# Delta-rule recurrence and expert layer on one core: eight units per substitution, a second transposition of K, and unread transposes on TensorE

## The chip, the cores and the metric

The kernel runs on one core of one Trainium2 chip. The metric is device time in microseconds, median over runs. Engines are named as in the profile: PE (TensorE matmuls), PEld (TensorE weight loads), DVE (VectorE), ACT (ScalarE), POOL (GpSimd), SP (SyncE, which here only issues DMAs). Everything is float32.

## The reference

Two blocks follow each other. The first is a delta-rule recurrence over 768 tokens for 4 batches of 8 heads of width 48. Keys are normalised, and a 48x48 state per head is updated token by token:

```
k_n = k / (norm(k) + 1e-6)
for t in range(768):
    y[t]  = q[t] @ state
    v_old = k_n[t] @ state
    state = state + beta[t] * outer(k_n[t], v[t] - v_old)
```

The second is a mixture of experts over the 3072 resulting rows of width 384. A cosine router picks one of eight experts for each row (argmax of normalised row times normalised expert embedding, over tau, with the softmax probability of the winner as gate), and the row becomes `gate * (relu(x @ w1[e]) @ w2[e])` with a hidden width of 1024.

## The kernel before

**Tiling of the recurrence.** The sequence is cut into 12 chunks of 64 tokens (C = 64, chunk m). A unit n = 2m + i is one chunk for two of the four batches and all their heads, so there are 24 units and two chains, i = 0 and 1, each with its own state S. Four units (two chunks, m = 2g and 2g + 1) are a group g; there are six. Inside a chunk the token-by-token update is a triangular system of size 64. It is split into halves of 32 (HC). The inverses of the 32x32 diagonal blocks are found by substitution on DVE: all blocks of a group lie one to a partition, and 30 steps of two instructions each (a product into tmp, a subtraction from X) work through them.

**Preparation of a group** (function `prepare`): K is loaded (`planned_k`, eight DMAs for a chunk), squared on ACT, summed on DVE, its root taken (ACT for groups 0 and 1, a POOL power later), scaled (`keys`, on POOL but for chunk 1), transposed on PE in eight 128x128 transposes (`transposes`, helper `turned`, L309), and copied out of PSUM by ACT into the K half of the buffer KQ. `gram_diag` forms the diagonal Gram blocks of a chunk from KQ in 64 small products of 48x32; `to_lanes` (L546) transposes them on DVE so that each block gets a partition; `lower` masks them on POOL; `product` (L561) and `subtract` (L565) are the substitution; `from_lanes` (L573) transposes back, and two ACT copies (`spread`) write W, which the group's units need for their solves.

**A unit** (function `unit`): a Gram of K against K and Q (PE), masked into Sx (ACT) and M (DVE, L652); then the chain: `old` (PE), R = V - old (DVE, L670), `solve` (PE), Y (ACT), `fix` (PE), U (ACT), `solve_again` (PE), Z (ACT), `update` (PE), state (DVE, L719). Beside it run `from_state` and `inside` (PE), which give the unit's output XC, its transposition, and the router's logits. After every fourth unit (twice at the end) `routing` chooses experts and puts tokens on lists in DRAM through POOL. `queries` loads and transposes q of a chunk into the Q half of KQ; `values` loads v and scales it on POOL into V (L615).

**Early tiles.** When the 16th unit is done, expert 0 already takes two tiles of 128 of its tokens (`early_tile`); their products are interleaved with the last units.

**What sets the order.** All of the recurrence is written as tasks, `plan.add(engine, busy, more, key, run, reads, writes, take, mode, hold)`: a planned busy time, a latency, a due time (key, in periods of 7.5 from the group's or unit's place), what it reads and writes, and whether it takes one of four PSUM pairs. `Plan.order` runs the tasks through its own list schedule and so fixes each engine's order; `emit` then issues the instructions in that order. Engines work their queues in order, so a waiting instruction holds what stands behind it. `with_warmers` holds a loop that never runs (`while False`), so no unread product is issued.

**The expert stage** starts when the recurrence's buffers are free: up to 31 tiles of 128 tokens, 26 of which run here, each a gather (POOL), a transposition, 24 and 8 products (PE), a ReLU copy (ACT), the gating (DVE) and a scatter (POOL). Weights stream through SP's queue.

Of the kernel before, what the change touches and what calls it, by code (L numbers as in the profile page):

```python
# [11 lines left out]
ALU = mybir.AluOpType  # L12
# [4 lines left out]
C = 64  # L17
HC = 32
T = 128
# [5 lines left out]
WARM = 0.45  # L25
# [3 lines left out]
class Plan:  # L29
# [77 lines left out]
    def with_warmers(self, order):  # L107
        out, last = [], 0.0
        for t, i in order:
            if self.tasks[i][0] == "PE":  # L110
                at = last + 0.15
                while False:
                    out.append((at, -1))
                    at += WARM
                last = self.ends[i]
            out.append((t, i))
        return sorted(out, key=lambda x: x[0])

    def emit(self, warm):
        free, left = list(range(len(self.psum))), dict(self.users)  # L120
        for _, i in self.with_warmers(self.order()):
            if i < 0:
                if free:
                    warm(self.psum[free[0]])
                continue
            _, _, _, _, run, _, take, of, _, _ = self.tasks[i]
            if take:
                self.held[take] = free.pop(0)
            run()
            for a in of:  # L130
                left[a] -= 1
                if not left[a]:
                    free.append(self.held[a])
# [6 lines left out]
def kernel(  # L140
# [80 lines left out]
    buffers("v", 3, [2, H, D])  # L221
    buffers("sq", 1, [2, H, D])
    buffers("K", 6, [2, H, C])
    buffers("KQ", 5, [2, NP, 2, 2 * C])
# [3 lines left out]
    rings["X"], rings["WT"] = carved(2, [HC, HC], w2_flat), carved(3, [HC, HC], w2_flat)[2:]  # L228
    buffers("tmp", 2, [(HC // 2) * (HC // 2)])
    buffers("W", 2, [HC, C])  # L230
# [93 lines left out]
    flat_buffers("V", 3, 4 * NP * D)  # L324
# [75 lines left out]
    def beta_refine(part):  # L400
# [5 lines left out]
             writes=["ident", "half", "iotas"] + [("K", i) for i in range(6)] + [("q", i) for i in range(2)])  # L406
# [14 lines left out]

    def prepare(g):
        ms = (2 * g, 2 * g + 1)
        t0 = group_key(g)
# [59 lines left out]
        for part in (slice(0, 1), slice(1, 2)) if g == 0 else (slice(0, 2),):  # L484
            xs = range(part.start, part.stop)
            those, roots_of = [at("rn", g) + (x,) for x in xs], [at("rt", g) + (x,) for x in xs]
            if g < 2:
                plan.add(*act(16 * len(xs)), t0 - 10 * PERIOD, roots_act(part), reads=those + ["half"], writes=roots_of)
            else:
                plan.add("POOL", 5.5, 0.2, t0 - 10 * PERIOD, roots(part), reads=those + ["half"], writes=roots_of)  # L490
            plan.add("DVE", 1.1 if g < 2 else 0.5, 0.2, t0 - 9.6 * PERIOD - (g == 0) * 30, scales(part), hold=g == 0,
                     reads=those, writes=roots_of + ["quots"])
            plan.add("DVE", 0.12 * len(xs), 0.2, t0 - 9.6 * PERIOD, scaled(part), hold=g == 0,
                     reads=[("sqb", 2 * g + x) for x in xs], writes=roots_of)

# [8 lines left out]
        def transposes(src, m, name):  # L504
            def step():
                turned(pair((name, m)), buf(src, m))
            return step

        def out_of_psum(m, name, cols):
            def step():  # L510
                act_copy(buf("KQ", m).rearrange("d i j y c -> d (i j y) c")[:, :, cols],
                         pair((name, m)).rearrange("d i (x c) -> d (i x) c", c=C))
            return step

        def gram_diag(m):
            def step_():
                p = pair(("diag", g))
                KQ = buf("KQ", m)
                for step in range(2 * NP):
                    for y in range(2):  # L520
                        for hf in range(2):
                            for jj in range(2):
# [6 lines left out]
                                mm(p[r:r + HC, jj, to:to + w], KQ[rows, i, j, y, hf * HC:(hf + 1) * HC], KQ[rows, i, j, y, c:c + w])  # L529
            return step_  # L530
        for m in ms:
            plan.add(*(dve(850) if m == 1 else pool(768)), t0 - 9.2 * PERIOD + (m % 2) * PERIOD, keys(m), hold=g == 0,
                     reads=[("k", m % 4, 0), ("k", m % 4, 1), at("rt", g) + (m % 2,)], writes=[at("K", m)])
            plan.add(*pe(8, 0.11), t0 - 8.6 * PERIOD + (m % 2) * PERIOD, transposes("K", m, "KT"), mode=2,
                     reads=[at("K", m), "ident"], take=("KT", m))
            plan.add(*act(1024), t0 - 8.4 * PERIOD + (m % 2) * PERIOD, out_of_psum(m, "KT", slice(0, C)),
                     reads=[("psum", ("KT", m))], writes=[at("KQ", m) + ("K",)])
        for m in ms:
            first = m % 2 == 0
            plan.add(*pe(64, 0.02), t0 - 7.2 * PERIOD, gram_diag(m), mode=1, reads=[at("KQ", m) + ("K",)],  # L540
                     writes=[("X_next", g % 2)] + ([] if first else [("psum", ("diag", g))]),
                     take=("diag", g) if first else None)
        X = buf("X", g)

        def to_lanes():
            nc.vector.transpose(X, pair(("diag", g)).rearrange("p jj (x c) -> p c jj x", c=HC))  # L546
        plan.add(*dve(1024), t0 - 6.5 * PERIOD, to_lanes, hold=g == 0, reads=[("psum", ("diag", g))],
                 writes=[at("X", g), ("X_next", g % 2)])
# [5 lines left out]
        plan.add("POOL", 1.2, 0.1, t0 - 6.4 * PERIOD, lower, writes=[at("X", g)])  # L554

        for j in range(1, HC - 1):
            rows = HC - 1 - j
            t = buf("tmp", j)[:, 0:rows * j].rearrange("p (a b) -> p a b", b=j)

            def product(j=j, rows=rows, t=t):  # L560
                nc.vector.tensor_tensor(t, X[:, j + 1:, j:j + 1].broadcast_to([128, rows, j]),  # L561
                                        X[:, j:j + 1, 0:j].broadcast_to([128, rows, j]), op=ALU.mult)

            def subtract(j=j, rows=rows, t=t):
                nc.vector.tensor_tensor(X[:, j + 1:, 0:j], X[:, j + 1:, 0:j], t, op=ALU.subtract)  # L565
            key = t0 - (6.0 - j * 4.0 / HC) * PERIOD
            plan.add("DVE", rows * j / 960 + 0.085, 0.13, key, product, reads=[at("X", g)], writes=[at("tmp", j)], hold=g == 0)
# [728 lines left out]
```

## Time and profile before

| | |
|---|---|
| median of 14 runs | 660.07 us (656.65 to 667.39) |
| the profiled execution | 658.53 us, of which the profile's span is 656.8 us |
| PE busy | 555.1 us, 85% of the span, 9995 instructions |
| DVE busy | 266.6 us, 41% |
| ACT busy | 180.3 us, 27% |
| POOL busy | 167.4 us, 25% |
| last product of the early tiles ends | 352.7 us |
| first product of the expert stage | 357.3 us |

Times in the profile count from the start of the span. A group line has the source line, engine, operation and tiles, the shape and number, then the busy time in us and the mean of one in ns, then the engine's idle time just before them and what ended it. PEclk is the share of TensorE's clock that was granted. A float32 product shows as two passes, so 16 products are x32; a transpose is one. Tile names that share storage are shown under one name: w_first stands for X as well as for K's load buffer, since both are carved from the first weights' storage.

### The profile page before, as it was taken

How to read it: one execution, taken by the hardware profiler on the slowest of the kernel's cores; microseconds unless marked ns; L12 is line 12 of the kernel's file. 1: busy time of each engine (PE TensorE's matmuls, PEld its weight loads, DVE VectorE, ACT ScalarE, POOL GpSimd, SP SyncE). 2: the span in 40 equal slices, each digit the busy share in tenths (PEclk: the TensorE clock that was granted, in tenths of full speed). 3: DMA queues.
4: the chain of work that ended last, by engine and by line, in shares of the span. 5: the costliest groups of instructions: out<-in, count | busy, mean ns of one | idle time of the engine just before them, and what ended most of it. 6: DMA issues, size and time to landing. Idle time of an engine off the chain costs nothing. (4 is left out here: it accounts for less than half of the span.)

```text
span 656.8 us, 22729 instructions
## 1 busy us (share of the span) xinstructions
PE 555.1 (85%) x9995; PEld 464.2 (71%) x9995; DVE 266.6 (41%) x749; ACT 180.3 (27%) x327; POOL 167.4 (25%) x217
## 2 busy tenths in 40 slices
PE   3563687777888887777996999999999999999991
PEld 3452676666787877676874878787878787878780
DVE  4798769679769777533214011111111111111100
ACT  2222625537427345263330101110101010101010
POOL 4434334354242121302203212121212121211100
PEclk9985769589869769799798999999999999999996
DMA  4444744534214311222002999999899999999600
GB/s 76 77 80 80 193 76 80 118 71 83 78 29 100 86 49 26 79 78 78 31 2 77 370 390 391 390 341 344 293 343 319 335 312 332 336 322 329 208 24 7
DMA packets 127911, 115.46 MB, mean 176 GB/s; under 512 B 83754, under 2 KB 113873, under 8 KB 127810
## 3 DMA queue, kind: packets, MB, share of 16 engines
q1 hardware_dynamic: 122242, 102.93, 51.0%
q0 software_dynamic: 4480, 10.85, 4.5%
q8 instruction: 80, 1.31, 0.8%
q10 hardware_dynamic: 1088, 0.20, 0.2%
q14 instruction: 21, 0.17, 0.1%
HBM read 102.02 MB, written 12.72 MB: 175 GB/s over the span
## 5 line engine op out<-in xcount | busy, mean ns | idle before, releaser
L1164 ACT ACTIVATE hT<-acc 128x512 f32<-128x512 f32 x52 | 31.1, 597 | 258.7 <-PE acc L1162 251.2
L1162 PEld LDWEIGHTS acc<-xTm,w 128*128 128x128 f32 x816 | 93.8, 192 | 4.5
L1162 PE MATMUL acc<-xTm,w 128*128 128x128 f32 x816 | 93.9, 275 | 0.0
L1169 PE MATMUL acc<-w,hT 128*128 128x384 f32 x272 | 90.5, 486 | 0.0
L1172 POOL DMA_INDIRECT out_dram<-y,ids x26 | 26.3, 1011 | 205.7 <-DVE y L1171 187.3
L1169 PEld LDWEIGHTS acc<-w,hT 128*128 128x128 f32 x272 | 50.4, 190 | 31.5
L273 PE MATMUL psum_pair<-KQ 48*32 48x64 f32 (+2 forms) x2304 | 53.5, 275 | 20.8 <-issue 10.4
L1154 DVE COPY xTm<-acc 128x384 f32<-128x384 f32 x26 | 14.5, 558 | 135.1 <-PE acc L1153 135.1
L565 DVE TENSOR_TENSOR w_first<-w_first,tmp 128x30 f32<-128x30 f32 (+9 forms) x180 | 67.8, 378 | 3.9
L561 DVE TENSOR_TENSOR tmp<-w_first 128x30 f32<-128x30 f32 (+9 forms) x180 | 66.8, 373 | 4.1
L1171 DVE TENSOR_SCALAR y<-acc,xg 128x384 f32<-128x384 f32 x26 | 16.1, 618 | 125.0 <-PE acc L1169 125.0
L273 PEld LDWEIGHTS psum_pair<-KQ 48*32 48x32 f32 (+1 forms) x2304 | 43.6, 139 | 28.7 <-issue 15.5
L1162 PEld LDWEIGHTS acc<-xTm,w_first 128*128 128x128 f32 x432 | 51.6, 198 | 3.3 <-DVE xTm L1154 1.2
L1162 PE MATMUL acc<-xTm,w_first 128*128 128x128 f32 x432 | 51.8, 282 | 0.8 <-DVE xTm L1154 0.8
L1169 PE MATMUL acc<-w_first,hT 128*128 128x384 f32 x144 | 47.9, 486 | 0.0
L273 PE MATMUL psum_pair<-S,KQ 48*64 48x64 f32 x1408 | 37.4, 247 | 10.0 <-issue 4.5
L273 PEld LDWEIGHTS psum_pair<-S,KQ 48*64 48x64 f32 x1408 | 31.7, 157 | 13.6 <-issue 6.8
L1169 PEld LDWEIGHTS acc<-w_first,hT 128*128 128x128 f32 x144 | 26.7, 190 | 16.7
L276 ACT ACTIVATE KQ<-psum_pair 128x1024 f32<-128x1024 f32 x24 | 24.4, 1023 | 47.1 <-PE psum_pair L309 34.3
L1137 POOL DMA_INDIRECT xg<-x_dram,ids x26 | 25.3, 975 | 38.5 <-DMA ids<-idmap 22.4
L960 POOL DMA_INDIRECT idmap<-tokid,slots_i x24 | 24.1, 1005 | 42.9 <-DVE slots_i L936 13.8
L615 POOL TENSOR_TENSOR V<-v,sqb 128x384 f32<-128x384 f32 x24 | 20.6, 863 | 51.1 <-DVE R L670 33.9
(183 smaller groups left out, 744.9 us busy)
## 6 DMA issues: line engine op xcount, KB each, us to landing
w<-in_moe_w_dram SPq DMA_DIRECT2D x34, 1536.0 KB
w_first<-in_moe_w_dram SPq DMA_DIRECT2D x16, 1536.0 KB
q<-in_q_dram SPq DMA_DIRECT2D x96, 48.0 KB
v<-in_v_dram SPq DMA_DIRECT2D x48, 96.0 KB
w_first<-in_k_dram SPq DMA_DIRECT2D x88, 48.0 KB
x_dram<-XC SPq DMA_DIRECT2D x5, 800.0 KB
idmap<-space SPq DMA_DIRECT2D x1, 2048.0 KB
w_first<-in_moe_w_dram SPq DMA_DIRECT2D x6, 256.0 KB
```

The lines of the kernel that those rows point to most:

```text
L273: nc.tensor.matmul(out_, lhsT=lhsT, rhs=rhs, start=start, stop=True, skip_group_check=True)
L276: nc.scalar.activation(out_, in_, ACT.Copy, scale=scale)
L561: nc.vector.tensor_tensor(t, X[:, j + 1:, j:j + 1].broadcast_to([128, rows, j]), X[:, j:j + 1, 0:j].broadcast_to([128, rows, j]), op=ALU.mult)
L565: nc.vector.tensor_tensor(X[:, j + 1:, 0:j], X[:, j + 1:, 0:j], t, op=ALU.subtract)
L615: nc.gpsimd.tensor_tensor(buf("V", m)[:, i * 2 * NP * D:(i + 1) * 2 * NP * D].rearrange("p (jj j d) -> p jj j d", jj=2, d=D), buf("v", m)[ ...
L960: put = nc.gpsimd.indirect_dma_start(out=idmap[:, :], out_offset=bass.IndirectOffsetOnAxis(ap=slot_i[:, i:i + 1], axis=0), in_=K["tokid"][ ...
L1137: t.read = nc.gpsimd.indirect_dma_start(out=t.x, out_offset=None, in_=x_dram[:, :], in_offset=bass.IndirectOffsetOnAxis(ap=t.ids[:, 0:1], ...
L1162: nc.tensor.matmul(psH[:, i, :], lhsT=t.w1[:, j, (f + i) * 128:(f + i + 1) * 128], rhs=t.xT[:, j, :], start=(j == 0), stop=(j == KC - 1))
L1164: nc.scalar.activation(t.hT[:, f:f + 4, :], psH, ACT.Relu)
L1169: nc.tensor.matmul(psO, lhsT=t.hT[:, f, :], rhs=t.w2[:, f, :], start=(f == 0), stop=(f == NF - 1))
L1171: nc.vector.tensor_scalar_mul(y, psO, t.x[:, Dm:Dm + 1])
L1172: nc.gpsimd.indirect_dma_start(out=out[:, :], out_offset=bass.IndirectOffsetOnAxis(ap=t.ids[:, 1:2], axis=0), in_=y, in_offset=None, bound ...
```

## The change

1. **Substitution of eight units at once.** Groups are solved in lanes `[[0], [1], [2, 3], [4, 5]]`. X becomes one tile with two halves, and for a pair each instruction covers both halves, so the 30 steps are issued four times and not six. Groups 2 and 3, and 4 and 5, are prepared together, ahead of the earlier one's first unit.
2. **K transposed separately for the diagonal Gram.** `prepare` transposes K into a buffer KT of its own (two of them, one carved from `space[0]`) for `gram_diag`; `queries` transposes K again, together with q, into KQ shortly before the chunk's units.
3. **Buffers.** v goes from three to two, V from three to two, KQ from five to three, tmp from two to one (twice as long), K from six to eight, W from two to three.
4. **Unread transposes.** `emit` looks at the plan: where PE is planned to wait more than 0.3 us before a task, and that task takes a PSUM pair or one is free, it issues up to six 128x128 transposes of the identity into that pair ahead of the task. Nothing reads them. In the built kernel these are 196 in 43 places.

```
-WARM = 0.45
+MOST = 6
...
-        free, left = list(range(len(self.psum))), dict(self.users)
-        for _, i in self.with_warmers(self.order()):
...
+        free, left, last = list(range(len(self.psum))), dict(self.users), 0.0
+        for t, i in self.order():
+            engine, _, _, _, run, _, take, of, _, _ = self.tasks[i]
             if take:
                 self.held[take] = free.pop(0)
+            if engine == "PE":
+                if t - last > 0.3 and (take or free):
+                    warm(self.psum[self.held[take] if take else free[0]], min(MOST, int((t - last) / 0.12)))
+                last = self.ends[i]
             run()
...
-    buffers("v", 3, [2, H, D])
+    buffers("v", 2, [2, H, D])
-    buffers("K", 6, [2, H, C])
-    buffers("KQ", 5, [2, NP, 2, 2 * C])
+    buffers("K", 8, [2, H, C])
+    buffers("KQ", 3, [2, NP, 2, 2 * C])
+    buffers("KT", 1, [2, NP, 2, C])
+    rings["KT"] += carved(1, [2 * NP, 2 * C], space[0])
-    rings["X"], rings["WT"] = carved(2, [HC, HC], w2_flat), carved(3, [HC, HC], w2_flat)[2:]
-    buffers("tmp", 2, [(HC // 2) * (HC // 2)])
-    buffers("W", 2, [HC, C])
+    X2, rings["WT"] = carved(1, [2, HC, HC], w2_flat)[0], carved(3, [HC, HC], w2_flat)[2:]
+    buffers("tmp", 1, [2 * (HC // 2) * (HC // 2)])
+    buffers("W", 3, [HC, C])
-    flat_buffers("V", 3, 4 * NP * D)
+    flat_buffers("V", 2, 4 * NP * D)
...
+    LANES = [[0], [1], [2, 3], [4, 5]]
+    lanes_of = {g: those for those in LANES for g in those}
...
-        t0 = group_key(g)
+        those = lanes_of[g]
+        t0 = group_key(those[0]) - (3.5 - those.index(g)) * (len(those) > 1) * PERIOD
...
+    def substitute(those):
+        two = len(those)
+        lo = those[0] % 2 if two == 1 else 0
+        X = X2[:, lo:lo + two]
+        names = [("X", lo + x) for x in range(two)]
+        t0, step = group_key(those[0]), (4.0 if two == 1 else 7.0) / HC * PERIOD
         for j in range(1, HC - 1):
             rows = HC - 1 - j
-            t = buf("tmp", j)[:, 0:rows * j].rearrange("p (a b) -> p a b", b=j)
+            n = two * rows * j
+            t = buf("tmp", j)[:, 0:n].rearrange("p (s a b) -> p s a b", s=two, b=j)
...
-                nc.vector.tensor_tensor(X[:, j + 1:, 0:j], X[:, j + 1:, 0:j], t, op=ALU.subtract)
+                nc.vector.tensor_tensor(X[:, :, j + 1:, 0:j], X[:, :, j + 1:, 0:j], t, op=ALU.subtract)
...
+        for src, first, of in (("K", 0, [at("K", m)]), ("q", C, [at("q", m) + (i,) for i in range(2)] + [("q", m % 2)])):
+            def transposes(src=src):
+                turned(pair((src, "T", m)), buf(src, m))
...
+            plan.add(*pe(8, 0.11), t0 - 3.5 * PERIOD + first / C, transposes, mode=2, reads=of + ["ident"], take=(src, "T", m))
...
-    prepare(0)
+    def prepare_lanes(those):
+        for g in those:
+            prepare(g)
+        substitute(those)
+        for g in those:
+            if g != 5:
+                out_of_lanes(g)
+    prepare_lanes([0])
...
-        if g + 1 < NG:
-            prepare(g + 1)
+        if g + 1 < len(LANES):
+            prepare_lanes(LANES[g + 1])
+        if g == 3:
+            out_of_lanes(5)
...
-    def warm(p):
-        for b in range(2):
-            mm(p[HALF[b], b, 0:256], ident[:, HALF[b]], half_wide)
+    def warm(p, n):
+        for _ in range(n):
+            nc.tensor.transpose(p[:, 0, 0:128], ident, ident)
     plan.emit(warm)
```

## The prediction

> **What bounds the kernel now.** I read the slices of the page first, for the stages; then the busy time in stretches, for the engine that is full in each; then the groups, for prices; then the timeline, for steps.
>
> ```profile
> PE   3563687777888887777996999999999999999991
> ...
> DVE  4798769679769777533214011111111111111100
> ...
> PEclk9985769589869769799798999999999999999996
> ```
>
> A slice is 16.4 us. DVE is busy six to nine tenths up to the 16th slice and almost idle from the 18th; PE is nearly full from the 23rd. The granted clock dips in the first half alone. So there are two stages: the recurrence up to 353 us, where the last early product ends, and the experts after it (304 us, PE 20.00 of 20 us in most stretches), which the change doesn't touch. What it is worth is how much earlier the first stage ends.
>
> Stretches (length; busy PE, PEld, DVE, ACT, POOL; then the granted clock):
>
> ```profile
> 90.00:96.00 6.00, 5.12 (x76) 4.67 (x79) 3.73 (x9) 1.09 (x2) 3.58 (x3) 0.50 0.51 90
> 180.00:186.00 6.00, 5.54 (x154) 5.05 (x155) 2.55 (x6) 1.02 (x1) 2.26 (x4) 0.50 0.20 37
> ...
> 198.00:204.00 6.00, 4.69 (x229) 4.25 (x228) 5.75 (x18) 4.68 (x6) 1.62 (x2) 1.00 0.32 56
> 228.00:234.00 6.00, 5.61 (x236) 4.90 (x236) 3.97 (x11) 1.52 (x2) 1.87 (x3) 0.50 0.52 124
> 258.00:264.00 6.00, 4.80 (x183) 4.51 (x177) 5.69 (x20) 3.57 (x8) 1.89 (x2) 1.00 0.01 3
> 288.00:294.00 6.00, 4.33 (x197) 3.89 (x197) 1.16 (x2) 4.25 (x11) 0.00 (x0) 1.00 0.13 37
> ```
>
> The bound changes hands. At 1.00 DVE is full (5.75, 5.69 of 6) and PE is not; at 0.50 PE is full and DVE waits (2.55, 3.97). In stretches of 1 us the clock is 0.50 in nine stretches before 353 us, 109 us in all. After 284 us, where the last substitution ends, neither is full: there the chain of a unit (PE, copy, PE, copy) sets the pace.
>
> Two sums measure this. **DVE:** its queue, priced by the rows' means with 33 ns between instructions, up to the last transposition of groups 0 to 5: 50.6, 92.9, 130.7, 165.9, 200.3, 235.8 us; the trace has them at 63.8, 113.7, 160.0, 201.4, 241.5, 284.2. So DVE waited 13, 21, 29, 36, 41, 48 us by then. **PE:** its queue to 353 us at full clock is 236 us by steps such as these:
>
> ```profile
> 183.03 1.99 PE L273 MATMUL psum_pair<-S,KQ 48*64 48x64 f32 x64
> 184.91 1.13 PE L273 MATMUL psum_pair<-R,W 64*64 64x64 f32 x32
> ...
> 329.76 0.69 PE L273 MATMUL psum_pair<-R,W 64*64 64x64 f32 x32
> 330.38 0.83 PE L273 MATMUL psum_pair<-enT,xT 128*128 128x8 f32 x6
> ...
> 339.18 0.49 PE L774 MATMUL psum_pair<-ident,XC 128*128 128x128 f32 x3
> 339.51 0.81 PE L1045 MATMUL psum_pair<-w_first,space 128*128 128x384 f32 x2
> ```
>
> From start to start a unit's 16 products (32 passes) take 0.62 us at full clock (329.76 to 330.38) and 0.94 at half (two groups in 1.88); three transposes take 0.33 us (339.18 to 339.51), so 0.11 each. From the first solve (67.9) to 353 us PE has 203 us of such work in 285; 87 us of these are at half clock, which at about 0.8 busy costs some 35 us, and 47 us are waits.
>
> **Substitution.** It goes from 360 DVE instructions to 240: groups 2 and 3 in one, 4 and 5 in one.
>
> ```profile
> L565 DVE TENSOR_TENSOR w_first<-w_first,tmp 128x30 f32<-128x30 f32 (+9 forms) x180 | 67.8, 378 | 3.9
> L561 DVE TENSOR_TENSOR tmp<-w_first 128x30 f32<-128x30 f32 (+9 forms) x180 | 66.8, 373 | 4.1
> ```
>
> ```profile
> L565 DVE TENSOR_TENSOR w_first<-w_first,tmp 128x240 f32<-128x240 f32 x12 | 5.9, 494 | 0.2
> L561 DVE TENSOR_TENSOR tmp<-w_first 128x240 f32<-128x240 f32 x12 | 5.3, 441 | 0.1
> L561 DVE TENSOR_TENSOR tmp<-w_first 128x30 f32<-128x30 f32 x12 | 2.3, 218 | 0.2
> L565 DVE TENSOR_TENSOR w_first<-w_first,tmp 128x30 f32<-128x30 f32 x12 | 2.1, 201 | 0.1
> ```
>
> From 30 to 240 elements costs 223 to 293 ns, 1.06 to 1.40 ns each; the rest is fixed. A mean instruction has 165 elements, so the doubled one takes 375 + 175 to 231 = 550 to 606 ns. A pair of groups: 60 x 0.55 to 0.61 = 33.0 to 36.4 us, against 120 x 0.375 = 45.1. Two pairs save 17 to 24 us, and 120 gaps of 33 ns 4 more: 21 to 28 us off DVE; I take 25. It does not come evenly, since groups 3 and 5 are now solved one group earlier. The changed DVE queue, priced alike, reaches the same marks at 57.2 (group 0), 92.7 (group 1), 147 and 149 (2 and 3), 205 and 207 (4 and 5). So up to unit 8 DVE has 16 us more to do than now, at unit 16 4 us more, and after that 29 us less.
>
> **K transposed twice.** PE gets 96 transposes (0.93 us per eight at 196.80: 11.3 us), ACT 12 copies of 1.02 us. ACT is busy 149 us of the first 360, so the copies hide; uncovered, they would cost 12 us. KQ goes from five buffers to three, v and V from three to two: POOL's V product then waits on the unit two chunks back (it waits 33.9 us for R now), and behind it in POOL stand K of chunks 8 to 11, wanted only by group 4's Gram, where I count 10 us of slack. One tmp costs nothing: one engine writes and reads it.
>
> **Unread transposes.** 196, in 43 places: 60 ahead of the first solve, 82 up to unit 8, 31 up to unit 16, 9 up to unit 23, 14 between the last results. At 0.11 us that is 21.6 us of PE, or 33 at the 0.17 that a transpose of K takes at the present mixture of clocks. On the path they cost between nothing (each in a wait, of which PE has 47 us after the first solve) and all of it; I take 6 us, as most stand before a task that takes a PSUM pair or a state, and the 14 at the end (1.5 us) in a queue that the trace shows without waits (347 to 352).
>
> What they give is the clock: between 0 and 35 us. The trace says when it falls. It changes on a grid of 3.41 us. Counting in each cell the streamed columns times the share of the array that a product fills (a full 128x128 transpose is 128), the eight falls after the first solve follow cells with 632 to 1393, and the rises cells with 1408 to 1872; three cells with 1228 to 1352 did not fall. So, as an estimate from these shapes, about 1400 decides. The Gram of one chunk (48x32 products) gives 768 in 1.9 us, so a stretch with Grams falls although PE is busy. Six unread transposes give 768 in 0.66 us. Spread over the 80 cells after the first solve, 136 of them and the second K transposes add some 350 a cell: enough for most of the five falls at 1008 to 1393, not for the three at 632 to 780. I take the half-clock time from 87 us to about 35.
>
> The Trainium skill ("TensorE: Matmul & The Clock Gate", Part 1) speaks against this part: the clock is halved only after an idle window of about 3.4 us. The longest PE wait after the first solve here is 2.4 us, so by the page the clock would not fall and the transposes would gain nothing; the rows at 180 and 228 us, 0.50 with PE busy 5.5 of 6, contradict it. By the page's rule the sum would be the DVE saving less 6 us.
>
> **The start.** 24 loads of K instead of 8 (some 0.65 us each to issue, 5.22 us for eight) now stand ahead of the first q in SP's queue: q and v come 10 us later, still ahead of their use (42 us). On PE the transposes of K of chunk 6 stand ahead of the first solve. Those wait for loads that SP has issued by 57 us, a landing of 2, square 0.84, sum 0.94, POOL's power 5.5 and product 1.6: 68 to 72 us. And the first W ends DVE's 57.2 + 13 of waits + 4.1 of ACT = 74. So the first solve is at 75 to 78, not 67.9: **8 us lost**.
>
> **Sum.** W of groups 2 and 3: 149 + waits of 18 to 29 (24) + 4 = 177, so unit 8's Y is at 178 (now 167.1). Unit 8 to 16: 61.2 us of PE queue; in the full-clock stretch from unit 14 to 17 PE got 20.7 of such us into 25.1 (0.82): 75 us, to 253 (now 258.7; W is there by 243). Unit 16 to 23: 60.1 us with DVE idle; units 20 to 22 did 12.6 in 14.0, so 0.87: 69, to 322 (now 330.5). Rest 20.3 at the 0.96 of now: 21, to 343; remaining half clock 2: 345. That is 8 us before 353. The profiled execution took 658.53, so 650.5; the median of the runs shown is 1.5 above it, so I give **652**.
>
> **Rivals.**
> 1. PE becomes the bound: slower. PE's queue grows by 33 us. If the clock falls as often as now and less than half of the 15 us of transposes after the first solve lie in waits, DVE's saving stands behind PE: 8 at the start + 16 more PE queue after it, less some 14 of waits filled: +10, **670**. For it: the start is lost in any case, and PE is full at 0.50. Against: 768 in each six transposes.
> 2. Unit 8's delay is not regained, since the units' pace comes from their own chain (9.6 us from unit 20 to 21 with DVE idle): no change, **660**.
> 3. Nearly no half clock, and DVE's waits shrink with it (23 of the 48 us that the trace has up to 241 us lie in half-clock stretches): unit 8 at 172, each later stretch 2 to 3 us shorter: -20, **640**.
>
> **Chances.** Forecast 0.46, rival 1 0.24, rival 2 0.13, rival 3 0.17. Faster by over 0.3% (2 us; about what a measurement of this kernel tells from no change): 0.63; within: 0.13; slower: 0.24. The ends of the unknown costs (transposes all on the path; all of 35 us of clock) reach a little past the rivals; 639 to 670 leaves out under 2 in 10.
>
> **What would show it.** Right: doubled instructions at 0.55 to 0.61 us; first Y at 76 to 79; a recurrence without substitution after about 240; half-clock time under 50 us; last early product near 345. Wrong: a clock row with as many dips (rival 1), unit 8's Y after 185, PE waiting for PSUM pairs at the unread transposes, or group 4's Gram late behind V in POOL.

## The result, and the profile after

| | before | after |
|---|---|---|
| median | 660.39 us (47 runs) | 693.83 us (686.75 to 697.82, 10 runs) |
| ratio, 95% interval | | 1.0485 (1.0452 to 1.0519) |
| profiled execution; its span | 658.53; 656.8 us | 691.92; 690.1 us |
| last product of the early tiles ends | 352.7 us | 387.0 us |
| from there to the span's end | 304.1 us | 303.1 us |

The change made the kernel slower by 33 us; 652 with a range of 639 to 670 was forecast. All of it is lost in the recurrence.

The page's slices of the changed kernel; a slice is 17.3 us here:

```profile
PE   5557867778779887889899799999999999999992
...
DVE  5799783578624885222321311111111111111100
...
PEclk9958896989955897988979899999999999999997
```

VectorE's row has two holes that it did not have before: the 7th slice (3) and the 12th (2). The clock row still dips, most at the 3rd, 12th and 13th slices (5 each). Half-clock time before the recurrence's end is 126.3 us, against 109.2, in one trace of each; among the runs of one kernel the mean granted clock varies by some 0.007, which is about 10 us of half clock.

The same stretches as in the prediction (length; busy PE, PEld, DVE, ACT, POOL; granted clock), now in the changed kernel:

```profile
90.00:96.00 6.00, 4.84 (x113) 4.45 (x110) 4.78 (x13) 2.76 (x6) 0.10 (x1) 1.00 0.40 69
180.00:186.00 6.00, 3.77 (x224) 3.17 (x226) 3.42 (x8) 4.41 (x5) 0.83 (x1) 1.00 0.51 94
198.00:204.00 6.00, 5.12 (x184) 4.42 (x187) 1.77 (x3) 0.49 (x1) 2.39 (x3) 0.50 0.02 5
228.00:234.00 6.00, 4.95 (x238) 4.50 (x234) 5.81 (x10) 3.33 (x8) 0.47 (x1) 0.88 0.25 44
258.00:264.00 6.00, 4.98 (x151) 4.20 (x143) 3.12 (x8) 0.43 (x1) 5.32 (x8) 0.68 0.58 155
288.00:294.00 6.00, 3.95 (x148) 3.03 (x147) 1.16 (x2) 2.29 (x6) 1.04 (x1) 1.00 0.65 147
```

At 198 us VectorE was full before (5.75); now it is busy 1.77 of 6, and at half clock TensorE is the busy one. One long stretch shows where the time went: 20 us to the recurrence's end, the kernel before and then the changed one.

```profile
20.00:352.70 332.70, 262.01 (x8101) 227.75 (x8101) 224.31 (x663) 142.44 (x264) 103.83 (x113) 0.84 0.33 75
```

```profile
20.00:387.00 367.00, 298.10 (x8374) 261.61 (x8372) 206.99 (x541) 154.76 (x275) 107.29 (x114) 0.83 0.30 68
```

The stretch is 34.3 us longer. TensorE is busy 36.1 us more (298.10 - 262.01), with the unread transposes (37.0 us in the whole span) as the largest new item, and its waits are 68.9 us in place of 70.7. VectorE did 17.3 us less, and the recurrence ended later all the same.

The groups of the substitution and the unread transposes in the changed kernel:

```profile
L562 DVE TENSOR_TENSOR tmp<-w_first 128x168 f32<-128x168 f32 (+28 forms) x120 | 57.7, 481 | 4.3 <-POOL w_first L545 1.4
L566 DVE TENSOR_TENSOR w_first<-w_first,tmp 128x168 f32<-128x168 f32 (+28 forms) x120 | 55.4, 461 | 2.9
...
L1112 PE MATMUL psum_pair<-ident 128*128 128x128 f32 x196 | 37.0, 327 | 19.9 <-DVE S L726 5.0
```

The substitution takes 113.1 us in place of 134.6, a doubled instruction 543 ns on the mean. So the saving on VectorE itself, 21.5 us of busy time, came as forecast (17 to 24), with instructions a little shorter than the 550 to 606 ns.

The Y copies of some units (us; the first product of a chain that needs W stands just ahead) show where the chain falls behind:

| kernel | unit 0 | 4 | 8 | 12 | 16 | 20 | 23 |
|---|---|---|---|---|---|---|---|
| before | 69.1 | 119.2 | 167.1 | 216.1 | 258.7 | 298.9 | 330.5 |
| after | 82.7 | 145.3 | 201.7 | 245.4 | 287.7 | 328.5 | 366.0 |

13.6 us are lost by the first solve, 26.1 by unit 4, 34.6 by unit 8; 5 us come back by unit 12, and 6 go again between unit 20 and unit 23. The timeline of TensorE in the changed kernel shows the first loss (start, time, operation):

```profile
70.86 1.50 PE L264 MATMUL psum_pair<-KT 48*32 48x64 f32 x126
...
72.20 1.48 PE L264 MATMUL psum_pair<-space 48*32 48x64 f32 x94
75.68 0.51 PE L264 MATMUL psum_pair<-space 48*32 48x64 f32 x32 [2.00 <-issue]
76.12 1.54 PE L1112 MATMUL psum_pair<-ident 128*128 128x128 f32 x6
77.59 1.56 PE L264 MATMUL psum_pair<-KQ 48*64 48x96 f32 x32
79.08 1.97 PE L300 MATMUL psum_pair<-ident,K 128*128 128x128 f32 x8
80.98 1.13 PE L264 MATMUL psum_pair<-V,W 64*64 64x64 f32 x32
```

W was complete at 73.5 us. The solve (V,W) started 7.5 us later, behind the diagonal Gram of group 2, six unread transposes, a unit's Gram and a transposition of K: work wanted by later units. Part of that work was late itself, since TensorE had stood for q before (its waits in the kernel before and in the changed one: in all, times, longest; then SP's issue of K that stands ahead of the first q):

```profile
PE psum_pair L309 <- DMA q<-in_q_dram: 4.0, 2, 2.1
```

```profile
PE psum_pair L300 <- DMA q<-in_q_dram: 14.3, 2, 10.1
16.58 17.03 SPq L285 DMA_DIRECT2D w_first<-in_k_dram  x24
```

The two long waits end at 38.1 and 43.4 us. The same waits sum to 14.3 to 17.6 us in all six kernels here that prepare groups 2 and 3 early with 24 loads of K ahead of q, and to at most 8.1 us in all others; what they cost by themselves no run separates.

Between unit 0 and unit 4 another 12.5 us are lost. Units 0 to 3 have their Y at 82.7, 95.9, 110.4 and 132.9 us, one after the other, where the kernel before has 69.1, 70.5, 96.8 and 99.6, two chains side by side; which part of the order set them apart is not shown. And the loss at unit 8:

```profile
183.53 0.99 PE L264 MATMUL psum_pair<-KT 48*32 48x64 f32 x75
185.52 0.71 PE L264 MATMUL psum_pair<-KT 48*32 48x64 f32 x53 [1.00 <-issue]
...
187.19 0.88 PE L264 MATMUL psum_pair<-space 48*32 48x64 f32 x66
189.35 0.78 PE L264 MATMUL psum_pair<-space 48*32 48x64 f32 x62 [1.29 <-issue]
...
190.69 0.54 PE L264 MATMUL psum_pair<-KT 48*32 48x64 f32 x34
194.45 1.49 PE L264 MATMUL psum_pair<-KT 48*32 48x64 f32 x94 [3.23 <-issue]
...
196.70 0.67 PE L264 MATMUL psum_pair<-space 48*32 48x64 f32 x31
197.91 1.52 PE L264 MATMUL psum_pair<-space 48*32 48x64 f32 x97 [0.54 <-issue]
199.36 1.12 PE L264 MATMUL psum_pair<-R,W 64*64 64x64 f32 x31
```

W of group 2 was there at 186.7, the solve (R,W) ran at 199.4, behind the four diagonal Grams of groups 4 and 5, which came in one bunch because their matrices' storage had just been freed. What the "issue" waits between the Gram's products are, nothing here shows.

### The profile page after: what moved, and what is told of

The parts are those of the page before. It is cut to its first block, busy times and chain, and to the rows that moved or that the text cites. A ratio compares the mean times of both kernels' runs of the same rounds, so it can differ in the third digit from the quotient of the medians.

```text
span 690.1 us, 23232 instructions
## 1 busy us (share of the span) xinstructions
PE 595.9 (86%) x10287; PEld 502.4 (73%) x10287; DVE 250.2 (36%) x629; ACT 192.7 (28%) x339; POOL 171.3 (25%) x218
## 5 line engine op out<-in xcount | busy, mean ns | idle before, releaser
L562 DVE TENSOR_TENSOR tmp<-w_first 128x168 f32<-128x168 f32 (+28 forms) x120 | 57.7, 481 | 4.3 <-POOL w_first L545 1.4
L566 DVE TENSOR_TENSOR w_first<-w_first,tmp 128x168 f32<-128x168 f32 (+28 forms) x120 | 55.4, 461 | 2.9
L1112 PE MATMUL psum_pair<-ident 128*128 128x128 f32 x196 | 37.0, 327 | 19.9 <-DVE S L726 5.0
L1112 PEld LDWEIGHTS psum_pair<-ident 128*128 128x128 f32 x196 | 26.5, 166 | 27.0 <-DVE S L726 5.9
L264 PE MATMUL psum_pair<-S,KQ 48*64 48x64 f32 x1408 | 39.1, 243 | 5.8 <-issue 5.6
L264 PEld LDWEIGHTS psum_pair<-S,KQ 48*64 48x64 f32 x1408 | 31.8, 152 | 12.2 <-issue 11.7
L622 POOL TENSOR_TENSOR V<-v,sqb 128x384 f32<-128x384 f32 x24 | 22.1, 926 | 71.3 <-DVE R L677 55.3
L300 PE MATMUL psum_pair<-ident,K 128*128 128x128 f32 x192 | 33.8, 339 | 0.7 <-DVE S L726 0.6
L1153 POOL DMA_INDIRECT xg<-x_dram,ids x26 | 25.3, 972 | 36.1 <-DMA ids<-idmap 22.4
```

Of the source, the lines that this page charges most:

```text
L264: nc.tensor.matmul(out_, lhsT=lhsT, rhs=rhs, start=start, stop=True, skip_group_check=True)
L300: nc.tensor.transpose(p[:, i, j * 128:(j + 1) * 128], two, ident)
L562: nc.vector.tensor_tensor(t, X[:, :, j + 1:, j:j + 1].broadcast_to([128, two, rows, j]), X[:, :, j:j + 1, 0:j].broadcast_to([128, two, row ...
L566: nc.vector.tensor_tensor(X[:, :, j + 1:, 0:j], X[:, :, j + 1:, 0:j], t, op=ALU.subtract)
L622: nc.gpsimd.tensor_tensor(buf("V", m)[:, i * 2 * NP * D:(i + 1) * 2 * NP * D].rearrange("p (jj j d) -> p jj j d", jj=2, d=D), buf("v", m)[ ...
L1112: nc.tensor.transpose(p[:, 0, 0:128], ident, ident)
```

## The experiments

The kernel before ran at 645 to 648 us on four of the chips used here and at 661 on a fifth, so results are ratios to the runs of before on the same chip. Expectations in us were put on the scale of 660. A time of a Y or of half clock comes from one profiled execution of its kernel. Some expectations count unread transposes; the traces hold 130 where they say 90, 158 where they say 103 and 66 where they say 38, spread up to the last results. Theories: **A**, the pairs cost (A1 by the order in which their early preparation stands on TensorE, A2 by VectorE having no other group to work on); **B**, the unread transposes cost; **C**, what remains costs (C1 the smaller rings, C2 the second transposition of K).

### Taking parts of the change away

**Without unread transposes** (`e1`).

```
-                if t - last > 0.3 and (take or free):
+                if False:
```

> The changed kernel without its 196 unread transposes; the planned order of all other work is the same, instruction for instruction. Theory A (the pairs: one storage for two groups' matrices leaves VectorE with one batch of substitution at a time, so that it idles at 104-131 and 182-202 us, and the loss is made there): 685-694 us, at most a few us better, VectorE's idle stretches still there. Theory B (the unread transposes: 37.0 us of TensorE busy and 19.9 us of its waits stand at them, ahead of tasks of the chain): 655-670 us. Theory C (the start and the smaller rings of v, V and KQ: the first solve 13.6 us later and the units 0 to 9 held by GpSimd's V): 685-694 us, with unit 0's Y still at 80-83 us. If the transposes do keep the clock up, the time is over 694 us and the half-clock time before 387 us is over 126 us.

Measured: 1.0484 (1.0378 to 1.0590). That is 692 on the scale of 660, out of B's range: within 0.01 the transposes are worth nothing either way in this kernel. Half-clock time was 153.6 us against 126.3 with them, but the time over 694 us that was to go with it did not show: what the clock gives, the transposes take again, as far as this measurement can tell.

**The kernel before with them** (`e2`: `emit` and `warm` of the change put into the kernel before).

> The kernel before with nothing of the change but the unread transposes: the planner sets 90 of them here, since its order has fewer planned waits. Theory A (pairs): 655-663 us, as the kernel before. Theory B (transposes): 90 of 196, so about half of the 33 us of the change is lost, 670-680 us. Theory C (start and rings): 655-663 us. If they keep the clock up, half-clock time before the recurrence's end falls from 109 us to under 95 us and the time is under 655 us.

Measured: 1.0061 (1.0026 to 1.0096). Half clock falls to 81.9 us, as the clock theory asked, and the time does not: it is 664 on the scale of 660, a little over the range of A and C and under B's. The loss is small, but clear of none.

**Every group alone** (`e3`), and **the same without unread transposes** (`e4`).

```
-    LANES = [[0], [1], [2, 3], [4, 5]]
+    LANES = [[g] for g in range(6)]
...
-            if g != 5:
-                out_of_lanes(g)
+            out_of_lanes(g)
...
-        if g == 3:
-            out_of_lanes(5)
```

> The changed kernel with every group of eight units substituted alone, as before (180 + 180 instructions of one group, two groups' storages in turn); the separate transposition of K, the rings and the unread transposes (103 here) stay. Theory A (pairs): VectorE has a second group to work on while it waits, 655-668 us, unit 8's Y at 165-172 us against 201.7. Theory B (transposes): 103 of 196 are left, 675-685 us. Theory C (start and rings): 685-694 us, GpSimd's V still waiting 12 us at 82-97 us.

> The changed kernel with every group alone and without unread transposes: what is left of the change is K's second transposition, the diagonal Gram from copies of its own, and the rings (v and V 2 each, KQ 3, K 8, W 3). Theory A (pairs): 655-668 us. Theory B (transposes): 655-668 us. Theory C (start and rings): 680-694 us. The second transposition's own price, by 12 x 0.94 us of TensorE, is at most 11 us, so 671 us is the most that A and B allow.

Measured: 1.0198 (1.0125 to 1.0271) and 1.0166 (1.0090 to 1.0242). That is 673 and 671 on the scale of 660, above A's ranges and below C's. So of 0.0485 the pairs are 0.032 (1.0484 - 1.0166, some 0.013 either way), what remains of the change 0.017, the transposes nothing that can be measured. A and C both hold a part; B fell. The granted clock is lower with the pairs too: without unread transposes and on one chip its mean is 0.8805 over the four runs with pairs and 0.9030 over the four without. How much of the 0.032 goes through the clock no run separates.

### Which pair, and which remainder

**One pair at a time**, without unread transposes (`e5`: `[[0], [1], [2, 3], [4], [5]]`; `e6`: `[[0], [1], [2], [3], [4, 5]]`).

> The changed kernel without unread transposes, with groups 2 and 3 in one substitution and groups 4 and 5 each alone. Both pairs without the transposes gave 1.048 times the kernel before, no pair 1.017: the pairs are worth 0.031. Theory A1 (a pair costs because the preparation of both its groups, four Grams and their transpositions, comes 3.5 periods earlier and stands in TensorE's order ahead of the units' chain; this pair's stands ahead of unit 0's solve): the larger part is here, 1.033-1.045, unit 0's Y at 80-82 us against 74. Theory A2 (a pair costs because VectorE has nothing to substitute while the pair waits for its second Gram, equally for both pairs): 1.030-1.034. The clock theory (bunched Grams of groups 4 and 5 at 183-199 us lower it): 1.017-1.025, with no stretch of half clock over 20 us after 180 us.

> The changed kernel without unread transposes, with groups 4 and 5 in one substitution and groups 2 and 3 each alone. Theory A1 (early preparation in TensorE's order): the smaller part, 1.018-1.030, unit 0's Y at 74-75 us, the units 0 to 8 as with no pair, a loss of 0-8 us between unit 8 and unit 16. Theory A2 (VectorE's filler): 1.030-1.034. The clock theory: 1.030-1.045.

Measured: 1.0391 (1.0325 to 1.0458) and 1.0338 (1.0283 to 1.0392). Each costs, 0.022 and 0.017 over none (together more than the 0.032 of both at once, but within the intervals). Unit 0's Y came at 84.9 with the first pair, 72.8 with the second alone: the late start belongs to the pair of groups 2 and 3, as A1 said, though A1's times were 80 to 82 and 74 to 75. The first size lies in A1's range, the second in A2's. The clock theory, by which only the second pair costs, fell.

**The rings of v and V** (`e7`: the kernel before with two of each; `e8`: single groups of the change with three of each, K six, W two).

```
-    buffers("v", 3, [2, H, D])
+    buffers("v", 2, [2, H, D])
...
-    flat_buffers("V", 3, 4 * NP * D)
+    flat_buffers("V", 2, 4 * NP * D)
```

> The kernel before with two buffers each for v and V in place of three, and nothing else of the change. Of the 0.017 that is left of the change without pairs and without unread transposes: theory C1 (the rings: GpSimd's V has to wait for the solve of the unit two chunks back, and what stands behind it in GpSimd's queue is late): 1.008-1.017. Theory C2 (the second transposition of K: 96 transposes and 12 ScalarE copies more): 0.997-1.003.

> The changed kernel with every group alone, without unread transposes, and with the rings of before where they fit: three buffers each for v and V, six for K, two for W; K's second transposition stays, with KQ of three and KT of two. Theory C1 (the rings of v and V): 1.000-1.008. Theory C2 (the second transposition): 1.013-1.020.

Measured: 1.0000 (0.9965 to 1.0036) and 1.0163 (1.0089 to 1.0238). The rings of v and V cost nothing that can be measured, and giving them back gains nothing. C1 fell. KQ had three buffers in `e8` too; its ring was not tried by itself.

### The substitution left out

In `e9` (pairs) and `e10` (single groups), and later in `e14` (the kernel before), the two instructions of a step become nothing (the second one, in `e14`):

```
-                nc.vector.tensor_tensor(X[:, j + 1:, 0:j], X[:, j + 1:, 0:j], t, op=ALU.subtract)
+                pass
```

> The changed kernel without unread transposes, and with all 240 VectorE instructions of the substitution left out: the matrices go back untransformed, so what the units compute is not the reference's, and the experts' stage may have other tiles; only the recurrence is read (its last product and the Y of the units). The planned order of everything else is unchanged. Beside it the same with every group alone. Theory A1 (what a pair costs is the early, bunched preparation in TensorE's order): the pairs stay 18-31 us behind the single groups at unit 23. Theory A2 (VectorE brings a pair's matrices late): without substitution the two end within 8 us of each other.

> The changed kernel with every group alone, without unread transposes, and with all 360 VectorE instructions of the substitution left out (the units do not compute the reference's result). With the substitution unit 23's Y came at 325 us here and at 356 us with the pairs. Theory A1: this one ends 18-31 us ahead of the pairs without substitution. Theory A2: within 8 us of it. By how far it ends before 325 us is what VectorE's substitution costs a kernel without pairs at all: 0-10 us if TensorE's queue is the bound, 30 us or more if VectorE is.

> The kernel before with all 360 VectorE instructions of the substitution left out (so the units do not compute the reference's result; the experts' stage may have other tiles, so the recurrence's end is read first); the planned order is unchanged. The prediction's reading (VectorE's substitution is what unit 8 and later groups wait for, and 25 us less of it is worth a good part of that): the recurrence ends 20 us or more earlier, 0.96-0.97. The rival (TensorE's queue is the bound, and the substitution lies beside it): 0-6 us earlier, 0.99-1.00.

Measured: unit 23's Y at 340.8 with pairs (356.4 with the substitution) and 322.6 with single groups (325.4). The two, one execution each, stay 18.2 us apart, of 31.0 with the substitution, at A1's edge: by these, the larger part of the pairs' price does not come from how long VectorE works. And the kernel before without any substitution is at 0.9962 (0.9923 to 1.0001) of itself. The long stretch of that kernel:

```profile
20.00:353.70 333.70, 264.93 (x8100) 232.02 (x8098) 103.56 (x301) 141.53 (x263) 101.17 (x112) 0.80 0.33 75
```

VectorE's 224.31 us have become 103.56, and the recurrence ends at 353.7, not a microsecond earlier. This execution had a lower clock in the stretch (0.80 against 0.84), but that is not what hides a gain: over all runs on this chip the mean granted clock is 0.892 without the substitution (10 runs) and 0.889 with it (13). Where the time of VectorE went, its waits show (20 to 300 us; waiting line, released by: us in all, times, longest), before and then without substitution:

```profile
DVE R L670 <- PE psum_pair L273: 14.9, 11, 2.5
DVE lz L785 <- PE psum_pair L273: 11.5, 7, 3.6
DVE S L719 <- PE psum_pair L273: 8.1, 6, 3.6
```

```profile
DVE R L669 <- PE psum_pair L273: 42.6, 16, 4.9
DVE lz L784 <- PE psum_pair L273: 41.9, 17, 4.9
DVE S L718 <- PE psum_pair L273: 27.7, 14, 4.5
```

The same three tasks of the units waited 34.5 us for TensorE, and wait 112.2 now. VectorE had been filling those waits with substitution. In the fullest stretches it was busy nearly 6 of 6 us and still not the bound. What could have told so beforehand are the lines of those who use W, the two solves in the kernel before (20 to 300 us; after the second bar, the idle time just ahead and who ended it):

```profile
L273 PE MATMUL psum_pair<-R,W 64*64 64x64 f32 x608 | 15.9, 251 | 2.4 <-ACT W L276 1.9 <-DVE R L670 0.6
...
L273 PE MATMUL psum_pair<-V,W 64*64 64x64 f32 x64 | 2.0, 314 | 3.1 <-ACT W L276 3.1
```

TensorE waited 1.9 + 3.1 = 5.0 us for W in the whole recurrence. Without substitution 2.5 us were gained (0.0038 of 660.7; the interval goes from 5 us to none).

### K's second transposition, doubled

From the single groups without unread transposes (1.0166): both parts twice (`e12`), the transposes alone (`e15`), the copies alone (`e16`).

```
-            return lambda: turned(pair(("early_KT", m)), buf("K", m))
+            return lambda: [turned(pair(("early_KT", m)), buf("K", m)) for _ in range(2)]
...
+                for _ in range(2):
                     act_copy(buf("KT", m).rearrange("d i j y c -> d i (j y c)"), pair(("early_KT", m)))
```

> The changed kernel with every group alone and without unread transposes, with each early transposition of K (8 transposes and one ScalarE copy, 12 times) made twice; the planned order is the same. Without the doubling it is at 1.017 times the kernel before. Theory C2a (the price of K's separate transposition is its own work in the queues of TensorE and ScalarE): the same price again, 1.028-1.036. Theory C2b (the work is hidden, and the price comes from the order that the planner makes of it or from KQ's three buffers): 1.015-1.022.

> The changed kernel with every group alone, without unread transposes, with the 96 early transposes of K made twice and their 12 ScalarE copies once. Without doubling it is at 1.017, with both doubled at 1.037. If the price of the second transposition is TensorE's work: 1.033-1.037. If it is ScalarE's copies (or the chain through both, where one alone would hide): 1.015-1.024.

> The changed kernel with every group alone, without unread transposes, with the 12 early copies of K's transposition (1.02 us each on ScalarE) made twice and the transposes once. If the price is TensorE's work: 1.015-1.021. If it is ScalarE's copies: 1.030-1.037.

Measured: 1.0371 (1.0315 to 1.0427), 1.0281 (1.0210 to 1.0352) and 1.0237 (1.0169 to 1.0306). Doubling both costs 0.0205, 13 us, with some 0.009 either way; 96 transposes alone 0.0115 and 12 copies alone 0.0071, each with some 0.010 either way. The transposes take 11.3 us of TensorE and the copies 12.2 of ScalarE. So the work as a whole is not hidden; C2b, by which it is, fell. How it divides stays open: either alone lies between the ranges for one queue only, and the price of the copies is not clear of none. A second doubling costs about as much as the 0.017 that was to be explained; that the first costs it in the same way (C2a) is inferred, with KQ's three buffers in all these kernels.

### The storage, and the place of the preparation

**A second storage for groups 2 and 3** (`e11`, and `e19` with both KT buffers). In `e11` the one KT buffer was written twice ahead of its first reading, so each group's first diagonal Gram used the second chunk's keys; instructions and order are whole, the output isn't the reference's.

```
+    X2b = ac.tile([128, 2, HC, HC], F32, name="X2b")
...
-        X = X2[:, half_of]
-        X_ = ("X", half_of)
+        second = 2 * (those == [2, 3])
+        X = (X2b if second else X2)[:, half_of]
+        X_ = ("X", half_of + second)
```

> The changed kernel without unread transposes, with a second storage of two groups' matrices for groups 2 and 3, so that groups 4 and 5 can be transposed in while 2 and 3 are still substituted; to make room KT has one buffer in place of two and Sx two in place of three. Theory A2 (VectorE idles at 182-202 us because the next pair may not enter): that stretch fills, 1.025-1.038 against 1.048. Theory A1 (early preparation in TensorE's order): groups 4's and 5's Grams come even earlier, 1.043-1.055.

> The changed kernel without unread transposes, with a second storage of two groups' matrices for groups 2 and 3 and both KT buffers; to make room M, Sx and Z have two buffers in place of three, which makes a unit's Gram wait for the unit two before it. The one storage as the main price of the pairs: 1.020-1.035 against 1.048, unit 23 20 us or more ahead of the pairs with one storage. The order of the early preparation as the main price: 1.043-1.055.

Measured: 1.0233 (1.0176 to 1.0290) and 1.0257 (1.0185 to 1.0329), against 1.0484 with one storage and 1.0166 with no pairs. So 0.023 to 0.025 of the pairs' 0.032 go away with a second storage, and with the order that the planner then makes; the two are not separated. A2's sizes (1.025 to 1.038) come nearest, but the stretch of 182 to 202 us did not fill (VectorE busy 9.7 of 20 us in `e11`, 7.4 in `e1`), and unit 23's Y came 15.2 us ahead of the pairs with one storage in `e19` (23.2 in `e11`), where 20 were expected. A1 as it was put, the order alone with the storage as it is, fell with this.

**The pairs' preparation 3.5 periods later** (`e17`).

```
-        t0 = group_key(those[0]) - (3.5 - those.index(g)) * (len(those) > 1) * PERIOD
+        t0 = group_key(those[0]) - (0.0 - those.index(g)) * (len(those) > 1) * PERIOD
```

> The changed kernel without unread transposes, with only the keys of the pairs' preparation moved 3.5 periods later, so that a pair's Grams are planned by the time its first group's own would be; the second Gram of groups 2 and 3 then stands behind unit 0's and 1's chain in TensorE's order. Theory A1 (order and early, bunched preparation): 1.025-1.042 against 1.048, unit 0's Y at 73-78 us. If the loss is in the pair's substitution coming late to VectorE: 1.050-1.065, since it starts later still.

Measured: 1.0465 (1.0388 to 1.0541), in neither range. The start is repaired, unit 0's Y at 71.1 and unit 4's at 125.0, and the loss comes back at unit 8 (184.8), as this timeline of TensorE shows:

```profile
171.32 0.84 PE L264 MATMUL psum_pair<-KQ 48*64 48x96 f32 x32
183.58 1.13 PE L264 MATMUL psum_pair<-R,W 64*64 64x64 f32 x32 [11.42 <-ACT W L267]
```

Now TensorE stands for 11.42 us because W is not there. So with one storage a pair gives only a choice: prepare early, ahead of the chain in TensorE's queue, or solve late. This is VectorE in the changed kernel, between the end of group 1 and the start of the first pair:

```profile
109.88 1.25 DVE L579 STREAM_TRANSPOSE w_first<-w_first 128x1024 f32<-128x1024 f32 x1
...
124.69 1.25 DVE L540 STREAM_TRANSPOSE w_first<-psum_pair 128x1024 f32<-128x1024 f32 x1 [6.04 <-PE psum_pair L264]
...
130.36 0.69 DVE L659 TENSOR_TENSOR M<-psum_pair,upper 128x512 f32<-128x512 f32 x1 [3.90 <-ACT Sx L267]
130.97 0.25 DVE L562 TENSOR_TENSOR tmp<-w_first 128x60 f32<-128x60 f32 x1
```

Group 3 needs the half of X that group 1 gives up at 109.88 (L579). Only then may its Gram run and be transposed in (L540, 124.69), and until then group 2, in its half since 76.3, may not be worked on either. The pair starts at 130.97, and its W comes at the end of 60 doubled instructions for both groups, 186.7 and 195.1, though group 3's is not wanted before unit 12. In the kernel before, group 2 entered at 88.4, ahead of group 1's end (112.5), and its W was ready at 164.1. With the second storage (`e11`) groups 2 and 3 entered at 88.5 and 99.1, and groups 4 and 5 at 150.7 and 187.9, against 190.2 and 199.6 in the changed kernel.

### Fewer unread transposes in the kernel before

**At most two ahead of a task** (`e18`: `MOST = 2` in `e2`'s kernel).

> The kernel before with unread transposes as in the change, but at most two (not six) ahead of a task that TensorE is planned to wait for: 38 in place of 90, all of them ahead of unit 4. With up to six the time was 1.006 of the kernel before, with 82 us of half clock. If a transpose costs by its number (0.006 x 38 / 90): 1.002-1.004. If two are enough to hold the clock and the rest only stood in the way: 0.990-0.998.

Measured: 1.0141 (1.0086 to 1.0197), with 95.6 us of half clock. Both expectations missed. The six runs lay between 649 and 661 us, four of them at 649 to 655, which is about 1.009 of the kernel before; so 66 cost no less than 130 did, and whether they cost more stays open. The clock was not held either: its mean over the runs is 0.900, against 0.903 of the kernel before on the same chip. No version that computes the reference's result beat the kernel before.

## Why the prediction was wrong

**The step that failed** is the one the sum stands on: "At 1.00 DVE is full ... and PE is not", and so "I take 25" us off VectorE as a gain to the groups after. VectorE was full in those stretches because it had work to fit into its waits for TensorE. The saving came (134.6 to 113.1 us of busy time), but the whole substitution is worth 0.0038, some 2.5 us (at most 5). I priced VectorE's queue and added its waits as if they were fixed (24 us); the experiment shows that they move: less work, more wait.

**The pairs.** The queue was priced by durations, "147 and 149", then 177 for W. W came at 186.7 and unit 8's Y at 201.7, not 178. What a pair demands of the order was left out: both Grams before the first step, a half that another group holds, and the next pair's four Grams in a bunch ahead of unit 8's solve. Price 0.032, 21 us at 660. This is the largest term. The sum had 11 us for it at unit 8 (178 against 167.1), all of it VectorE's, and took them back in the stretches after; for TensorE's order and for the storage it had nothing.

**The second transposition.** Its 11.3 us of TensorE were counted rightly, and 0.0166 of 660 is 11 us; but the sum has no line of its own for it, and forecasts the stretches from unit 8 to 16 and 16 to 23 shorter than before (75 and 69 us against 91.6 and 71.8). That the ScalarE copies "hide" is neither shown nor refuted: doubled alone they cost 0.0071, with 0.010 either way. That v and V of two buffers cost nothing was right (1.0000).

**The unread transposes.** 6 us on the path and half-clock time from 87 to 35 us after the first solve were taken; the net was nothing measurable in the changed kernel, and half clock before the recurrence's end did not fall (126.3 us against 109.2 in the two traces). The prediction spread the transposes' columns evenly over the cells, "some 350 a cell", but they stand in 43 places, and the bunched Grams left long half-clock stretches: the longest, 37.5 us from 191.9, follows a cell of the 3.41-us grid with 912 columns of the full array and TensorE busy 1.87 of 3.40 us. The rule for the clock itself fits most cells: of 13 falls in the changed kernel, 10 follow cells with under 1400 such columns and three follow 1552 to 1633; all 13 rises follow 1456 or more. Four cells with 1146 to 1376 did not fall, and three with 1476 to 1552 did not rise, so about 1400 is a rough mark.

**The start.** W at 73.5 (forecast 74), but the first Y at 82.7, not 76 to 79: I saw K of chunk 6 ahead of the solve, not group 2's Gram. And q was not "still ahead of their use": TensorE waited 14.3 us for it, at 28 to 43 us, with what the first units need in its queue behind.

**The stretches.** Unit 8 to 16 took 86.0 us (forecast 75), 16 to 23 78.3 (69), the rest 21.0 (21). Rival 1 named the side, and the bound to which the runs point, TensorE's longer queue at a clock that falls as often, 670; it too was short, by the pairs.

## What to carry to other kernels

A busy engine is a bound only if somebody waits for what it makes: read the idle time ahead of the consumers (5.0 us here) before you credit a saving on the producer, and leave the work out once to see what it is worth at most. When two pieces of work are joined into one instruction, the first waits for the input of the second and is done with its end, and the storage of both is taken together, so count when each may enter and who used to work in between. On the engine that the rest waits for, do not count extra work as hidden (K's transposition and its copies, doubled, cost 13 us), and do not count a higher clock as a gain before the work that raises it is paid: here it never paid.

## What the runs showed of the hardware

The clock falls without an idle window. These are three neighbouring cells of the changed kernel (length; busy PE, PEld, DVE, ACT, POOL; granted clock):

```profile
297.70:301.10 3.40, 3.40 (x30) 3.19 (x31) 1.97 (x12) 2.58 (x6) 0.00 (x0) 1.00 0.02 5
301.10:304.50 3.40, 2.62 (x86) 2.34 (x88) 1.02 (x5) 1.05 (x2) 2.94 (x4) 1.00 0.48 163
304.50:307.90 3.40, 2.96 (x83) 2.60 (x76) 0.14 (x1) 0.00 (x0) 2.81 (x5) 0.50 0.86 254
```

TensorE was busy 2.62 of 3.40 us on small products (1196 columns of the full array), with no wait over 0.4 us, and the next cell is at 0.50. The Trainium skill ("TensorE: Matmul & The Clock Gate", Part 1) has the clock halved after an idle window of about 3.4 us; these rows show it halved without one, and so do the rows of the prediction.

The unread transposes do raise the granted clock. Its mean over the runs is 0.9175 with them (10 runs) and 0.9040 without (13) in the kernel before, and 0.9245 and 0.9030 with single groups (4 runs each), all on one chip; with pairs it is 0.9042 (12 runs) and 0.8805 (4), on two chips. In none of the three did the time fall.
